# First layer's output product of four blocks as seven block products in phases of its own

## The chip, the cores and the metric

The kernel runs on one core of a Trainium2 chip. The metric is the device time of one execution in microseconds. Five engines of the core appear in the profile: TensorE (PE, with its weight loads as PEld), VectorE (DVE), ScalarE (ACT), GpSimd (POOL), SyncE (SP, which issues DMAs).

## The reference, cut to what matters

```python
def reference(**kw):
    attn = _attn_ref(q, k, v, mem_k, mem_v)              # batch 4, heads 8, sequence 768, head 64
    x = attn.transpose(0, 2, 1, 3).reshape(3072, 512)
    gate = 1.0 / (1.0 + np.exp(-(x @ w_gate)))            # first layer: 512 -> 1536 -> 512
    x = gate * (x @ w_val) @ w_out
    h = x @ w_in                                          # second layer: 512 -> 2048 -> 512
    P = a[0] + a[1] * h + a[2] * h**2 + a[3] * h**3
    Q = 1.0 + abs(b[0]) * abs(h) + abs(b[1]) * h**2
    return P / (Q + 1e-06) @ w_out2
```

The attention takes chunks of 32 queries with a context of 16 to the left and 8 to the right, and 8 memory keys in front. All is in fp32.

## The kernel before

An fp32 product is made of three matmuls in a shorter format: each operand is split into a high part (a ScalarE copy with rounding) and a low part (a VectorE subtraction), and TERMS multiplies high by high, high by low, low by high. A matmul takes 128x128 of weights and 512 columns of tokens. The 3072 tokens lie in six blocks of 512; the first layer's 1536 features in NF1 = 12 tiles of 128.

Every instruction goes through a `Recorder`, whose `emit` (line 485) is the line that all rows of the trace show; tiles tell them apart. `plan()` keeps TensorE's order as the code writes it, and sorts the instructions of ScalarE, VectorE and the DMA queues by costs and by due times counted back from the matmuls that need them. Each engine works its list in order.

Phase 1 does attention and the first layer of blocks 0 and 1 feature tile by feature tile: `gate_val`, then `out1(j, f)`, the output product ("visit") of one tile: 4 banks acc0 to acc3 x 3 terms = 12 matmuls, accumulating over the 12 tiles. Blocks (2, 3) and (4, 5) are then taken in pairs by `quads(ja, s0)`: for each of six feature pairs fp and for m = 0 (gate) and 1 (value), `quad` makes the 2 x 2 block product (two feature halves by two halves of tokens and of depth) with seven products for eight, by sums and differences of operands. A half is 7 products x 6 matmuls = 42. There are four PSUM banks for it (tiles p_fp_m_0 to 3); products 0 to 3 start a bank each, products 4, 5 and 6 add to banks 0, 2 and 3 after these have been read once. VectorE adds the banks up (u, v, c12, c21, c22); ScalarE takes the sigmoid; `done` multiplies by the gate: for block ja the result is split at once (`g_split`), for block jb it is kept unsplit (`g_held`) until later. Weights of the products are either plain ("a", from DRAM tensor wqa, split) or combined ("s", from wqs, where `w_comb_hi`, `w_comb_lo` and `w_comb_store` put them in split form, 512 KB each).

The visits of block ja stand between the halves (`visit(run)`, at all but the second half); those of block jb have a phase: for block 3 `outs(3, ...)`, mixed with attention of blocks 4 and 5; for block 5 the start of the second layer's task list: `visit1`, 10 of them pure (the last two of block 4 among them), and four inside the first three quads of the second layer, at the places LATE. A quad has two places for a visit, one ahead of its fifth product and one ahead of its last but one; filled are the first place of all three quads and the second of the third. The second layer takes three pairs of blocks, 8 quads each (tiles q_X, q_Y, q_Z).

## Time and profile before

| | us |
|---|---|
| Runs | 1134.87, 1133.35, 1133.77 (median 1133.77) |
| Span of the profiled execution | 1131.7 |
| Busy PE, DVE, ACT, POOL | 1120.1 (99%), 870.7 (77%), 746.8 (66%), 23.1 (2%) |
| DMA queue q1, share of 16 engines | 74.4% |
| Quads of blocks 2 and 3 | 254 to 402 |
| Output phase of block 3 | 402 to 453 |
| Quads of blocks 4 and 5 | 453 to 594 |
| Last visits of block 4, visits of block 5 | 594 to 624, the last four between 629 and 664 |
| Second layer | 624 to the end |

The runs are timed from outside the span, so they lie some 2 us above it. An engine's share is an average over stages; what an engine waits for in a stage is read from the timeline and the waits.

### The profile page before, as it was taken

To read this page: it belongs to the slowest core of one execution; us is meant where nothing else is said; L and a number is where in the kernel's file an instruction comes from. 1 tells how busy PE (TensorE), PEld (TensorE's weight loads), DVE (VectorE), ACT (ScalarE), POOL (GpSimd) and SP (SyncE) were. 2 spreads that over 40 slices of the span, in tenths; PEclk is the share of its full clock that TensorE was granted. 3 is DMA by queue.
4 is the path that set the end of the run, shared out by engine and by line. 5 is a ranking of instruction groups with operands and counts; after the bars stand their busy time and mean duration, and the time that the engine had idled before them with its cause. 6 is when DMAs were issued, how large, how long until landed. Compare 5 with 4: busy or idle time off the path is not lost.

```text
span 1131.7 us, 20049 instructions
## 1 busy us (share of the span) xinstructions
PE 1120.1 (99%) x7815; PEld 918.8 (81%) x7815; DVE 870.7 (77%) x1180; ACT 746.8 (66%) x1129; POOL 23.1 (2%) x39
## 2 busy tenths in 40 slices
PE   8999999999999999999999999999999999999998
PEld 4888888888888888888888788888888888888887
DVE  4788867764676767565667499999899999899982
ACT  5999565653355466343345599875799874898852
POOL 0000000000000000000000000000000000000000
PEclk8999999999999999999999999999999999999999
DMA  9899799997988899898967487679686689686682
GB/s 370 314 351 367 256 344 355 336 391 254 371 274 316 297 382 386 311 366 301 320 234 267 170 249 208 223 259 333 188 257 196 216 288 316 176 268 206 199 256 95
DMA packets 100319, 318.79 MB, mean 282 GB/s; under 512 B 10752, under 2 KB 11008, under 8 KB 100224
## 3 DMA queue, kind: packets, MB, share of 16 engines
q1 hardware_dynamic: 96192, 303.51, 74.4%
q0 software_dynamic: 3456, 12.58, 6.3%
q8 instruction: 62, 1.02, 0.4%
q10 hardware_dynamic: 576, 1.41, 0.3%
q14 instruction: 33, 0.27, 0.1%
HBM read 240.91 MB, written 63.96 MB: 269 GB/s over the span
## 4 chain that ended last, share of the span: by engine, by line
PE 95%; issue 2%; DMA 1%; ACT 1%; DVE 1%; POOL 0%; ACTq 0%; POOLq 0%; DVEq 0%
PE acc L485 40%; PE p L485 20%; PE h L485 12%; PE q_X L485 10%; PE q_Z L485 5%; PE q_Y L485 3%; PE xp L485 2%; PE sp L485 2%; PE tp L485 1%; DMA q<-u 1%; PE idle L485 1%; DMA k<-k_in 1%; ACT u L485 0%; DVE q L485 0%; DVE s L485 0%
## 5 line engine op out<-in xcount | busy, mean ns | idle before, releaser
L485 PE MATMUL acc<-w2o,G 128*128 128x512 f32 x1152 | 268.4, 389 | 0.0
L485 PEld LDWEIGHTS acc<-w2o,G 128*128 128x128 f32 x1152 | 216.3, 188 | 44.9
L485 PE MATMUL acc<-g,wp 128*128 128x512 f32 x720 | 177.2, 394 | 0.0
L485 PEld LDWEIGHTS acc<-g,wp 128*128 128x128 f32 x720 | 133.2, 188 | 28.7 <-issue 0.4
L485 PE MATMUL q_X<-x,wi 128*128 128x512 f32 x576 | 146.7, 390 | 2.2 <-ACT hb L485 2.0
L485 PE MATMUL p<-b,wpq_s 128*128 128x512 f32 x576 | 138.3, 389 | 0.0
L485 PE MATMUL h<-x,wp 128*128 128x512 f32 x576 | 137.5, 392 | 0.0
L485 PEld LDWEIGHTS q_X<-x,wi 128*128 128x128 f32 x576 | 107.8, 188 | 26.0 <-ACT hb L485 3.2
L485 PEld LDWEIGHTS p<-b,wpq_s 128*128 128x128 f32 x576 | 108.1, 188 | 22.5
L485 PEld LDWEIGHTS h<-x,wp 128*128 128x128 f32 x576 | 107.4, 188 | 22.4
L485 ACT ACTIVATE st<-st 128x512 f32<-128x512 f32 (+1 forms) x124 | 77.2, 673 | 0.0
L485 PE MATMUL p<-x,wpq_a 128*128 128x512 f32 x288 | 73.1, 389 | 0.0
L485 PE MATMUL q_Z<-x,wi 128*128 128x512 f32 x288 | 73.1, 389 | 0.0
L485 PEld LDWEIGHTS p<-x,wpq_a 128*128 128x128 f32 x288 | 54.1, 188 | 11.3
L485 PEld LDWEIGHTS q_Z<-x,wi 128*128 128x128 f32 x288 | 54.0, 188 | 11.3 <-DVE hb L485 0.2
L485 DVE SCALAR_TENSOR_TENSOR q<-q,u 128x1024 f32<-128x1024 f32 x48 | 58.4, 1219 | 3.9 <-ACT u L485 3.7
L485 DVE SCALAR_TENSOR_TENSOR t<-t,cf,u 128x1024 f32<-128x1024 f32 x48 | 61.4, 1279 | 0.1
L485 ACT ACTIVATE u<-q,qc 128x1024 f32<-128x1024 f32 x48 | 54.6, 1146 | 8.3 <-DMA q<-u 6.4
L485 ACT ACTIVATE G<-hb 128x512 fp32r<-128x512 f32 x48 | 29.9, 628 | 34.7 <-PE acc L485 29.4
L485 ACT ACTIVATE u<-u 128x1024 f32<-128x1024 f32 x48 | 50.3, 1055 | 0.4
L485 ACT ACTIVATE hb<-q_X 128x512 f32<-128x512 f32 x48 | 28.4, 592 | 32.0 <-PE q_X L485 32.0
L485 DVE TENSOR_TENSOR c<-u,p 128x512 f32<-128x512 f32 x39 | 26.8, 686 | 26.8 <-PE p L485 26.7
(290 smaller groups left out, 1703.4 us busy)
## 6 DMA issues: line engine op xcount, KB each, us to landing
w2o<-w2o SPq DMA_DIRECT2D x96, 512.0 KB, 4.6
wi<-wq SPq DMA_DIRECT2D x72, 512.0 KB, 4.8
st<-w_in SPq DMA_DIRECT2D x62, 512.0 KB, 6.8
wp<-wqa SPq DMA_DIRECT2D x55, 512.0 KB, 6.3
wpq_s<-wqs SPq DMA_DIRECT2D x48, 512.0 KB, 8.2
wpq_a<-wqa SPq DMA_DIRECT2D x36, 512.0 KB, 7.3
wqa<-wp SPq DMA_DIRECT2D x30, 512.0 KB, 6.8
v<-v_in SPq DMA_DIRECT2D x24, 512.0 KB, 6.3
```

Source lines behind the costliest of these rows:

```text
L485: getattr(getattr(self.nc, t.eng), op)(*[real(x) for x in args], **{n: real(x) for n, x in kw.items()})
```

## The change

The output product of blocks 2 to 5 is now taken per pair, as a 2 x 2 block product with seven products. The gated values of a pair are kept unsplit in four groups, "11", "12", "21", "22" (parity of the feature tile, block); `g_tile` gives them room. Each of the seven products (OUTS: the bank it goes to, the weights' slot, the operand) is taken in three steps k of four tiles, 12 matmuls each. A step is `o_weights` (one load of 512 KB), `o_split` (high part on ScalarE, low part on VectorE, 1024 columns each), for some `o_pre` (subtractions of 1024 columns that make the combined operands in place) and `o_mm`; `o_sum` copies or adds a bank when a product is done. X is the product that others continue in its banks.

Three steps (EARLY) run inside the quads, behind halves 5, 6 and 9. The other 18 (STEPS) come in an order of their own behind the quads: for blocks 2 and 3 with the attention of later blocks (`outs(2, O1, STEPS)`), for blocks 4 and 5 with 12 of them ahead of the second layer and six (LATE) at both places of its first three quads. Between the halves of the quads no visit is left, except the last one of block 1 and the three early steps.

The output weights are stored as eight slots per feature pair in a new tensor wqo; four of them are sums made in phase 1 (`o_whole`, `o_comb`, `o_store`). The combined gate and value weights go to wqs unsplit (256 KB); `w_comb_hi` and `w_comb_lo` are gone from phase 1, and each of the 48 loads in the quads is followed by its own high and low part. The steps of the attention for blocks 4 and 5 and of the second layer's weights have new places, and two tiles of x swap pools.

```diff
     def w_comb_store(i):
-        store_split(("s", i), wqs[i])
-        del wp["s", i]
+        nc.sync.dma_start(out=wqs[i], in_=sf[i])
...
-            src = wqa[2 * fp + w[1], w[2]] if w[0] == "a" else wqs[4 * fp + w[1]]
-            load_split(quad_key(ja, fp, w), src)
+            key = quad_key(ja, fp, w)
+            if w[0] == "a":
+                load_split(key, wqa[2 * fp + w[1], w[2]])
+                continue
+            t = split_tile(key)
+            hi, lo = t[:, 0], t[:, 1]
+            nc.sync.dma_start(out=lo.bitcast(F32), in_=wqs[4 * fp + w[1]])
+            nc.scalar.activation(out=hi, in_=lo.bitcast(F32), func=ACTF.Copy)
+            nc.vector.tensor_tensor(out=lo, in0=lo.bitcast(F32), in1=hi.bitcast(F32), op=ALU.subtract)
...
-            if j == jb:
-                nc.vector.tensor_tensor(out=g_held(j, f), in0=sg, in1=y, op=ALU.mult)
-                return
-            nc.vector.tensor_tensor(out=sg, in0=sg, in1=y, op=ALU.mult)
-            g_split((1, j, f), sg, 512)
+            o = f"{1 + f % 2}{1 + j - ja}"
+            nc.vector.tensor_tensor(out=g_held(ja, o, fp), in0=sg, in1=y, op=ALU.mult)
         tag = f"{ja}_{fp}_{m}"
         product(0)
...
         product(4)
         done(ja, f0, None)
         fill()
@@ -1023,18 +1035,25 @@
         add(c12, u, bank[2])
         done(jb, f0, c12)
         product(6)
-        c21 = t2(f"c21_{tag}")
-        add(c21, u, bank[3])
-        done(ja, f1, c21)
+        add(u, u, bank[3])
+        done(ja, f1, u)
...
+    def g_held(ja, o, fp):
+        return g_tile(ja, o, fp // 2)[:, fp % 2]
...
+    OUTS = (
+        ("X", 0, "11"),
+        ("Y", 2, "21"),
+        ("X", 4, "t2"),
+        ("Z", 5, "12"),
+        ("X", 7, "11"),
+        ("Z", 3, "21"),
+        ("X", 6, "22"),
+    )
+    ow, og, ob, osum = {}, {}, {}, {}
+    def flat(ap):
+        return ap.rearrange("p a n -> p (a n)")
+    def o_weights(ja, i, k):
+        t = ow[ja, i, k] = wpool.tile([P, 2, 512], F32R, tag="w", name=f"ow{ja}_{i}_{k}")
+        nc.sync.dma_start(out=t.bitcast(F32), in_=wqo[2 * k : 2 * k + 2, OUTS[i][1]].rearrange("f p n -> p f n"))
+    def o_sub(out, x0, x1):
+        nc.vector.tensor_tensor(out=flat(out), in0=flat(x0), in1=flat(x1), op=ALU.subtract)
+    def o_pre(ja, k, what):
+        for w in what:
+            if w == "1":
+                o_sub(g_tile(ja, "11", k), g_tile(ja, "12", k), g_tile(ja, "11", k))
+            elif w == "3":
+                o_sub(g_tile(ja, "12", k), g_tile(ja, "22", k), g_tile(ja, "12", k))
...
+    def o_split(ja, i, k):
...
+        hi, lo = (wpool.tile([P, 2, 512], F32R, tag="w", name=f"o{b}{ja}_{i}_{k}") for b in "hl")
+        nc.scalar.activation(out=flat(hi), in_=flat(src), func=ACTF.Copy)
+        nc.vector.tensor_tensor(out=flat(lo), in0=flat(src), in1=flat(hi).bitcast(F32), op=ALU.subtract)
+        og[ja, i, k] = hi, lo
+    def o_sum(ja, i, r):
+        tag = f"{ja}_{i}_{r}"
+        name, _, _ = OUTS[i]
+        bank = ob[ja, name, r]
+        def copy():
+            t = t2(f"os{tag}")
+            nc.scalar.activation(out=t, in_=bank, func=ACTF.Copy)
+            return t
+        def add(t):
+            nc.vector.tensor_tensor(out=t, in0=t, in1=bank, op=ALU.add)
+            return t
+        if i in (0, 2, 3):
+            osum[ja, i, r] = copy()
+        elif i == 1:
+            held.append((ja, r, add(osum.pop((ja, 0, r)))))
+        elif i == 4:
+            held.append((ja + 1, 2 + r, add(osum.pop((ja, 3, r)))))
+        elif i == 5:
+            held.append((ja, 2 + r, add(osum.pop((ja, 2, r)))))
+        else:
+            held.append((ja + 1, r, copy()))
+    def o_mm(ja, i, k):
+        name = OUTS[i][0]
+        w, x = ow.pop((ja, i, k)), og.pop((ja, i, k))
+        last = k == NF1 // 4 - 1
+        for r, f in ((r, f) for r in range(2) for f in range(2)):
...
+            for t, (a, b) in enumerate(TERMS):
+                c = 256 * a + P * r
+                nc.tensor.matmul(
+                    ob[ja, name, r],
+                    lhsT=w[:, f, c : c + P],
+                    rhs=x[b][:, f],
+                    start=(i in (0, 1, 3) and k == 0 and f == 0 and t == 0),
+                    stop=(last and f == 1 and t == 2),
+                    skip_group_check=True,
+                )
+            if last and f == 1:
+                o_sum(ja, i, r)
+    EARLY = [(0, 0), (1, 0), (0, 1)]
+    STEPS = [(0, 2), (1, 1), (1, 2)] + [(i, k) for i in range(2, len(OUTS)) for k in range(NF1 // 4)]
...
+    def o_whole(f):
+        t = so[f] = t2(f"so{f}")
+        hi, lo = (halves(wp[1, 1, f, 2], b).bitcast(F32) for b in range(2))
+        nc.vector.tensor_tensor(out=t.rearrange("p (m c) -> p m c", m=2), in0=hi, in1=lo, op=ALU.add)
+    def o_comb(fp):
+        t = [so.pop(2 * fp + i) for i in range(2)]
+        (a11, a21), (a12, a22) = ([x[:, 256 * m : 256 * m + 256] for m in range(2)] for x in t)
+        for out, x0, x1, op in (
+            (a22, a21, a22, ALU.add),
+            (a21, a11, a21, ALU.subtract),
+            (a11, a22, a11, ALU.subtract),
+            (a12, a12, a11, ALU.subtract),
+        ):
+            nc.vector.tensor_tensor(out=out, in0=x0, in1=x1, op=op)
+        for i in range(2):
+            split_out_hi(("so", fp, i), t[i])
+            split_out_lo(("so", fp, i), t[i])
+    def o_store(fp):
+        for i in range(2):
+            store_split(("so", fp, i), out_slots(fp, 4 + 2 * i))
+            del wp["so", fp, i]
...
+        EARLY_AT = dict(zip((5, 6, 9), EARLY))
+        def early(ja, i, k):
+            o_weights(ja, i, k)
+            o_split(ja, i, k)
+            o_pre(ja, k, "13" if i == 0 else "24x")
+            o_mm(ja, i, k)
         def quads(ja, s0):
             for i in range(NF1):
@@ -1474,35 +1621,41 @@
                 store1_end()
                 if m == 0 and fp < NF1 // 2 - 1:
                     quad_load(ja, fp + 1, 0, AHEAD)
-                if i:
-                    load_out(1 if fp < NF1 // 2 - 1 else 3)
                 run(*STORES)
                 run(*LOADS)
                 quad(ja, fp, m, lambda: run(attn_exp, conv2_hi, conv2_lo, conv2))
                 run(conv2_bits, comb2, pair_sum)
                 run(done2)
-                if i != 1:
-                    visit(run)
+                if (ja, i) == (2, 0):
+                    out1(*steps[-1])
+                if i in EARLY_AT:
+                    early(ja, *EARLY_AT[i])
+                run(pair_qk, pair_max)
                 run(pair_t)
-        def outs(j, s0, fn, n=NF1 + 1):
-            for i in range(n):
-                run = runner(s0 + i)
-                load_out(1)
+        def out_step(ja, i, k):
+            store1_end()
+            o_weights(ja, i, k)
+            if (i, k) == (2, 0):
+                o_pre(ja, k, "2")
+            o_split(ja, i, k)
+            if i < 2:
+                o_pre(ja, k, "13" if i == 0 else "24")
+            o_mm(ja, i, k)
+        def outs(ja, s0, steps):
+            for n, (i, k) in enumerate(steps):
+                run = runner(s0 + n)
                 run(quad_load)
                 run(*LOADS)
                 run(*STORES)
-                store1_end()
-                for nxt in visits[nv + 2 : nv + 3]:
-                    if nxt[0] == j:
-                        g_split((1, *nxt), g_held(*nxt), 512)
-                fn(i)
                 run(x_comb, attn_exp)
                 run(x_comb_hi, conv2_hi, conv2)
-                visit(run)
+                out_step(ja, i, k)
+                run(pair_out, pair_qk, pair_max)
                 run(pair_t)
                 run(x_comb_lo, conv2_lo, conv2_bits, comb2, pair_sum)
-                run(done2, conv2_keep)
+                run(done2)
...
-        outs(3, O1, lambda i: None)
+        outs(2, O1, STEPS)
         quads(4, Q2)
...
-        n5 = 10
-        for i, (j, f) in enumerate(todo1):
-            ready1(j, f)
-        for i, (j, f) in enumerate(todo1[:n5]):
-            visit1(j, f)
+        LATE = 6
+        for i, k in STEPS[: len(STEPS) - LATE]:
+            out_step(4, i, k)
         for i in range(4):
             load2i(0, 0, i)
-        late = list(todo1[n5:])
-        LATE = (4, 2, 0, 5, 3, 1)[: len(late)]
+        late = STEPS[len(STEPS) - LATE :]
...
-                    elif i in LATE:
-                        visit1(*late.pop(0))
+                    elif late:
+                        out_step(4, *late.pop(0))
+                        if not late:
+                            store1_end()
```

How the order moves shows at three places. The first is TensorE in the quads of blocks 4 and 5, at the seam between the two halves of the third feature pair (p_2_0 and p_2_1 are the banks, x and b the operands, wpq the weights). Before:

```order
L485 MATMUL p_2_0_2_5890<-b_5096,wpq_2_s_5809 128x512 x6
L485 MATMUL p_2_0_3_5907<-b_5279,wpq_2_a_1_5822 128x512 x6
L485 MATMUL acc_0_5740<-g_4_2_5836,wp_4_2_2_5473 128x512 x3
L485 MATMUL acc_1_5746<-g_4_2_5836,wp_4_2_2_5473 128x512 x3
L485 MATMUL acc_2_5753<-g_4_2_5836,wp_4_2_2_5473 128x512 x3
L485 MATMUL acc_3_5759<-g_4_2_5836,wp_4_2_2_5473 128x512 x3
L485 MATMUL p_2_1_0_5965<-x_0_4907,wpq_2_a_0_5712 128x512 x6
L485 MATMUL p_2_1_1_5976<-b_5121,wpq_2_s_5709 128x512 x6
```

and after:

```order
L485 MATMUL p_2_0_0_5868<-x_1_4869,wpq_2_a_1_5748 128x512 x6
L485 MATMUL p_2_0_2_5898<-b_5299,wpq_2_s_5745 128x512 x6
L485 MATMUL p_2_0_3_5912<-b_5407,wpq_2_a_1_5775 128x512 x6
L485 MATMUL p_2_1_0_5959<-x_0_4864,wpq_2_a_0_5697 128x512 x6
L485 MATMUL p_2_1_1_5972<-b_5199,wpq_2_s_5632 128x512 x6
L485 MATMUL p_2_1_2_5989<-b_5157,wpq_2_s_5628 128x512 x6
```

The visit of 12 matmuls (acc, with g and wp) is gone; the next half stands directly behind the one before.

The second is the end of the quads of blocks 4 and 5. On TensorE, before:

```order
L485 MATMUL p_5_1_0_6546<-x_1_4916,wpq_5_a_1_6350 128x512 x6
L485 MATMUL p_5_1_2_6577<-b_5096,wpq_5_s_6365 128x512 x6
L485 MATMUL p_5_1_3_6585<-b_5279,wpq_5_a_1_6389 128x512 x6
L485 MATMUL acc_0_5740<-g_4_9_6453,wp_4_9_2_6076 128x512 x3
L485 MATMUL acc_1_5746<-g_4_9_6453,wp_4_9_2_6076 128x512 x3
L485 MATMUL acc_2_5753<-g_4_9_6453,wp_4_9_2_6076 128x512 x3
L485 MATMUL acc_3_5759<-g_4_9_6453,wp_4_9_2_6076 128x512 x3
```

and after:

```order
L485 MATMUL p_5_1_0_6524<-x_1_4869,wpq_5_a_1_6349 128x512 x6
L485 MATMUL p_5_1_2_6550<-b_5299,wpq_5_s_6324 128x512 x6
L485 MATMUL p_5_1_3_6560<-b_5407,wpq_5_a_1_6374 128x512 x6
L485 MATMUL ob_X_6049<-oh_0_2_6600,ow_0_2_6463 128x512
L485 MATMUL ob_X_6049<-ol_0_2_6605,ow_0_2_6463 128x512
L485 MATMUL ob_X_6049<-oh_0_2_6600,ow_0_2_6463 128x512 x2
```

The visit of tile 9 stood behind the last half; now a step whose operand oh_0_2 and ol_0_2 come from the last half does.

On VectorE at the same place (v, c, u: sums of banks; gh: held gated values; g: those for a split), before:

```order
L485 TENSOR_TENSOR v_5_1_6592<-v_5_1_6592,p_5_1_3_6585 128x512
L485 TENSOR_TENSOR gh_2_6411<-c_4_5_0_6503,v_5_1_6592 128x512
L485 TENSOR_TENSOR c_4_5_0_6503<-c_4_5_0_6503,p_5_1_0_6546 128x512
L485 TENSOR_TENSOR c_4_5_1_6617<-p_4_5_1_6573,p_5_1_2_6577 128x512
L485 TENSOR_TENSOR g_4_10_6609<-c_4_5_0_6503,g_4_10_6609 128x512
L485 TENSOR_TENSOR gh_2_6411<-c_4_5_0_6520,c_4_5_1_6617 128x512
L485 TENSOR_TENSOR xf_0_1_0_6625<-p_4_5_1_6573,p_5_1_3_6585 128x512
L485 TENSOR_TENSOR c_4_5_0_6520<-c_4_5_0_6520,xf_0_1_0_6625 128x512
L485 TENSOR_TENSOR g_4_11_6641<-c_4_5_0_6520,g_4_11_6641 128x512
```

and after (ot, ol: combined operand and low part for the steps):

```order
L485 TENSOR_TENSOR v_5_1_6569<-c_4_5_0_6520,p_5_1_2_6550 128x512
L485 TENSOR_TENSOR ol_2_0_6571<-ot_0_6490,oh_2_0_6548 128x1024
L485 TENSOR_TENSOR v_5_1_6569<-v_5_1_6569,p_5_1_3_6560 128x512
L485 TENSOR_TENSOR ot_1_6580<-gh_22_0_5660,gh_11_0_5669 128x1024
L485 TENSOR_TENSOR gh_11_1_6418<-v_5_0_6498,p_5_1_0_6524 128x512
L485 TENSOR_TENSOR v_5_1_6569<-c_4_5_0_6520,p_5_1_2_6550 128x512
L485 TENSOR_TENSOR gh_22_1_6410<-v_5_0_6498,v_5_1_6569 128x512
L485 TENSOR_TENSOR gh_12_1_6435<-c_4_5_0_6520,v_5_1_6569 128x512
L485 TENSOR_TENSOR ol_0_2_6605<-gh_11_1_6418,oh_0_2_6600 128x1024
```

Operations of 1024 columns now stand between the sums, and the low part ol_0_2 behind the last products of the gate.

The third is TensorE in the second layer's second quad, before:

```order
L485 MATMUL q_1_Z<-x_0_3_6718,wi_1_1_6860 128x512 x6
L485 MATMUL q_1_X<-x_0_2_6735,wi_1_1_6860 128x512 x6
L485 MATMUL acc_5_0_6691<-G_5_9_6848,wv_9_6874 128x512 x3
L485 MATMUL acc_5_1_6699<-G_5_9_6848,wv_9_6874 128x512 x3
L485 MATMUL acc_5_2_6707<-G_5_9_6848,wv_9_6874 128x512 x3
L485 MATMUL acc_5_3_6713<-G_5_9_6848,wv_9_6874 128x512 x3
L485 MATMUL q_1_X<-x_0_1_6664,wi_1_2_6896 128x512 x6
L485 MATMUL q_1_X<-x_0_22_6743,wi_1_2_6896 128x512 x6
L485 MATMUL q_1_Z<-x_0_4_6749,wi_1_3_6918 128x512 x6
```

and after, from the second place on:

```order
L485 MATMUL q_1_X<-x_0_1_6753,wi_1_2_6945 128x512 x6
L485 MATMUL ob_X_6049<-oh_6_0_6909,ow_6_0_6950 128x512
L485 MATMUL ob_X_6049<-ol_6_0_6957,ow_6_0_6950 128x512
L485 MATMUL ob_X_6049<-oh_6_0_6909,ow_6_0_6950 128x512 x2
L485 MATMUL ob_X_6049<-ol_6_0_6957,ow_6_0_6950 128x512
L485 MATMUL ob_X_6049<-oh_6_0_6909,ow_6_0_6950 128x512
L485 MATMUL ob_X_6058<-oh_6_0_6909,ow_6_0_6950 128x512
L485 MATMUL ob_X_6058<-ol_6_0_6957,ow_6_0_6950 128x512
L485 MATMUL ob_X_6058<-oh_6_0_6909,ow_6_0_6950 128x512 x2
L485 MATMUL ob_X_6058<-ol_6_0_6957,ow_6_0_6950 128x512
L485 MATMUL ob_X_6058<-oh_6_0_6909,ow_6_0_6950 128x512
L485 MATMUL q_1_X<-x_0_22_6726,wi_1_2_6945 128x512 x6
```

Before, a visit stood at the first of the two places and none at the second, between q_1_X<-x_0_1 and q_1_X<-x_0_22; now a step stands at both.

## Rows read from the trace of the kernel before

**Rows 1.** The page: span, busy time of each engine, DMA in all.

```profile
span 1131.7 us, 20049 instructions
PE 1120.1 (99%) x7815; PEld 918.8 (81%) x7815; DVE 870.7 (77%) x1180; ACT 746.8 (66%) x1129; POOL 23.1 (2%) x39
...
DMA packets 100319, 318.79 MB, mean 282 GB/s; under 512 B 10752, under 2 KB 11008, under 8 KB 100224
```

**Rows 2.** The chain of waits, 263 to 297 us: start, length in us, what.

```profile
263.43 2.72 PE acc L485 x12
266.15 19.04 PE p L485 x84
285.19 2.72 PE acc L485 x12
287.91 9.52 PE p L485 x42
```

**Rows 3.** Stages: window, length, then busy us of PE, PEld, DVE, ACT, POOL, clock, DMA share, GB/s.

```profile
139.00:254.00 115.00, 115.00 (x1360) 95.28 (x1359) 82.00 (x128) 70.75 (x119) 0.34 (x2) 1.00 0.97 356
254.00:402.00 148.00, 148.00 (x1137) 122.07 (x1136) 97.41 (x145) 65.93 (x103) 0.49 (x3) 1.00 0.86 307
402.00:453.00 51.00, 51.00 (x714) 42.40 (x713) 35.08 (x57) 36.58 (x67) 0.00 (x0) 1.00 1.02 380
453.00:594.00 141.00, 141.00 (x624) 116.75 (x623) 82.83 (x138) 53.97 (x92) 0.00 (x0) 1.00 0.86 307
594.00:624.00 30.00, 30.00 (x134) 24.82 (x133) 22.88 (x37) 16.75 (x29) 0.00 (x0) 1.00 0.75 274
624.00:700.00 76.00, 73.96 (x324) 60.30 (x323) 60.29 (x62) 62.09 (x76) 3.62 (x4) 1.00 0.66 204
700.00:1100.00 400.00, 399.86 (x1765) 330.81 (x1764) 374.32 (x406) 316.63 (x399) 17.39 (x20) 1.00 0.75 241
```

**Rows 4.** TensorE's waits (total, times, longest), then its timeline at the second layer's start.

```profile
PE q_X L485 <- ACT hb L485: 2.0, 2, 1.4
...
634.37 1.65 PE L485 MATMUL q_X<-x,wi 128*128 128x512 f32 x6 [0.69 <-ACT hb L485]
...
648.26 1.67 PE L485 MATMUL q_X<-x,wi 128*128 128x512 f32 x6 [1.35 <-ACT hb L485]
```

**Rows 5.** Timeline of VectorE in the second layer: start, length in us, operation.

```profile
662.36 1.22 DVE L485 SCALAR_TENSOR_TENSOR q<-q,u 128x1024 f32<-128x1024 f32 x1
663.50 0.68 DVE L485 TENSOR_TENSOR hb<-hb,q_Z 128x512 f32<-128x512 f32 x1
664.10 1.28 DVE L485 SCALAR_TENSOR_TENSOR t<-t,cf,hb 128x1024 f32<-128x1024 f32 x1
```

**Rows 6.** Timeline of TensorE, the bare seam of blocks 2 and 3.

```profile
274.15 1.52 PE L485 MATMUL p<-b,wpq_a 128*128 128x512 f32 x6
275.51 1.52 PE L485 MATMUL p<-x,wpq_a 128*128 128x512 f32 x6
```

**Rows 7.** Timeline of all engines, at 404 and at 584 us.

```profile
404.53 1.03 PE L485 MATMUL tp<-ident,s 128*128 128x128 f32 x8
...
584.57 1.52 PE L485 MATMUL p<-x,wpq_a 128*128 128x512 f32 x6
...
586.12 0.60 ACT L485 ACTIVATE p<-p 128x512 f32<-128x512 f32 x1 [0.17 <-PE p L485]
```

**Rows 8.** Groups by shape: ScalarE's 1024-column pass (busy us, mean ns | idle before).

```profile
L485 ACT ACTIVATE u<-u 128x1024 f32<-128x1024 f32 x48 | 50.3, 1055 | 0.4
```

**Rows 9.** DMA issues: out<-in, count, KB each, median us to landing.

```profile
wi<-wq SPq DMA_DIRECT2D x72, 512.0 KB, 4.8
wi<-wq SPq DMA_DIRECT2D x24, 256.0 KB, 4.7
```

More of the change, by code (lines that the diff above doesn't have):

```diff
@@ L830, in split_lo, with halves, split_out_hi, split_out_lo @@
         nc.vector.tensor_tensor(out=t[:, 1], in0=src, in1=t[:, 0].bitcast(F32), op=ALU.subtract)
+    def halves(t, b):
+        return t.rearrange("p m (b c) -> p m b c", b=2)[:, :, b]
+    def split_out_hi(key, src):
+        t = split_tile(key)
+        nc.scalar.activation(out=halves(t, 0), in_=src.rearrange("p (m c) -> p m c", m=2), func=ACTF.Copy)
+    def split_out_lo(key, src):
+        hi, lo = (halves(wp[key], b) for b in range(2))
+        src = src.rearrange("p (m c) -> p m c", m=2)
+        nc.vector.tensor_tensor(out=lo, in0=src, in1=hi.bitcast(F32), op=ALU.subtract)
+    def out_slots(fp, i):
+        return wqo[fp, i : i + 2].rearrange("m p n -> p m n")
     def store_split(key, dst):
@@ L1134, in pv @@
         if n0 == 0 and (j < 2 or j % 2 == 0):
-            xt[j] = [x_tile(f"x{j}_{h}") for h in range(2)]
+            xt[j] = [
+                b_tile(f"x{j}_{h}", F32R, [P, 2, 2, 512]) if j >= 4 else x_tile(f"x{j}_{h}") for h in range(2)
+            ]
             if j >= 2:
@@ L1247, in fused_kernel @@
         at(s0, w_comb, i)
-        at(s0, w_comb_hi, i)
-        at(s0, w_comb_lo, i)
         at(s0 + 1, w_comb_store, i)
+    for f in range(NF1):
+        at(NF1 + f, o_whole, f)
+        if f % 2:
+            at(NF1 + f, o_comb, f // 2)
+            at(NF1 + f + 1, o_store, f // 2)
     for t in range(4, NPAIR, 2):
@@ L1452, in fused_kernel @@
             run(pair_sum)
-            run(w_comb_lo, x_comb_lo, conv2_lo, conv2_bits, comb2)
+            run(x_comb_lo, conv2_lo, conv2_bits, comb2)
             run(done2)
-        visits = [steps[-1]] + [(j, f) for j in range(PAIRS[0][0], NB1) for f in range(NF1)]
-        n_out, nv = 1, 0
-        def load_out(n):
-            nonlocal n_out
-            for v in visits[n_out : n_out + n]:
-                w1_load(*v, OUT)
-            n_out += n
-        def visit(run):
-            nonlocal nv
-            out1(*visits[nv], mid=lambda: run(pair_out, pair_qk, pair_max))
-            nv += 1
+        EARLY_AT = dict(zip((5, 6, 9), EARLY))
[4 more added lines that the diff above has]
+            o_mm(ja, i, k)
         def quads(ja, s0):
```

133 lines of the change are left out of this document (66 added, 67 removed).

## The prediction

> **What bounds the kernel now.** I read the page's busy table first: TensorE is busy 99% of the 1131.7 us span, VectorE 77%, ScalarE 66% [rows 1]. The chain of waits agrees; inside the quads it is nothing but TensorE work, 9.52 us for the 42 matmuls of a half and 2.72 us for the 12 of a visit, one straight behind the other [rows 2]. So a 512-column matmul costs 2.72 / 12 = 226.7 ns on the path that sets the end. The table by stage then tells what lies beside TensorE where the change works [rows 3]: in the quads of blocks 2 and 3 (254 to 402 us) VectorE is busy 97.4 of 148 us, in block 3's output phase (402 to 453) 35.1 of 51, in the quads of blocks 4 and 5 (453 to 594) 82.8 of 141, in block 5's visits (594 to 624) 22.9 of 30. TensorE is busy to the last hundredth in all four, at a granted clock of 1.00. The one place nearby where TensorE waits is the start of the second layer: 2.0 us in two waits for ScalarE [rows 4]. So a matmul taken away pays in full, as long as VectorE and the loads, which get more to do, keep up. Most of the working below is about that.
>
> **Removed: matmuls.** Of the 864 rows for the first layer's output product, 288 (blocks 0 and 1) stay. The four other blocks had 4 x 12 visits x 12 = 576; now two pairs have 7 products x 3 steps x 12 = 252 each, 504 in all. 72 matmuls fewer, 72 x 0.2267 = **-16.3 us** on the path. The gate and value matmuls (24 halves of 42) keep their number.
>
> **Added: VectorE's work.** Dense rows show that VectorE starts an operation of 1024 columns 1.14 us after the one before (662.36 to 663.50) though it lasts 1.22, and one of 512 columns 0.60 us after (663.50 to 664.10) though it lasts 0.68 [rows 5]. With these I count the operations of each stage from the order, wide and narrow ones, without the 128x1 ones:
> - Quads of blocks 2 and 3: 14 wide and 125 narrow before, 14 x 1.14 + 125 x 0.60 = 91 us (the trace has 97.4 busy with the overlap counted); after, 26 and 133, 109 us. TensorE has 148 us there now; eight visits go (three early steps come for eleven visits, and block 1's last visit stays), and the attention scores of a later stage come in, about 131 us. VectorE at 84%.
> - Output phase of blocks 2 and 3: 55 narrow, 33 us; after, 22 and 42, 50 us, beside 18 steps x 2.72 = 49 us of output products and some 15 us of attention. 78%.
> - Quads of blocks 4 and 5: 127 narrow, 76 us; after, 14 and 147, 104 us, beside 12 x 9.52 + 3 x 2.72 = 122.4 us. 85%; the tightest feature pair is the third, 22.0 us against 21.8.
> - From there to the first product of the second layer: 35 narrow, 21 us; after, 16 and 27, 34.4 us, beside 12 x 2.72 = 32.6 us.
> - Elsewhere small changes (the 12 output weights' sums and splits in the first phase, about 10 us, where VectorE has 82.0 of 115 [rows 3]).
>
> In all VectorE gets about 92 us more, some 960 of 1118. It is below TensorE in every stage but the fourth. I price this at nothing, except where the order makes TensorE wait. Cover if I am wrong there: none, every microsecond shows.
>
> **The seams between halves.** Before, a visit of 2.72 us lay between nearly all halves, and 2 seams were bare; after, 13 are, 5 in the first pair and 8 in the second. Both bare ones of before show no gap: the half that ends at 275.51 [rows 6], and the 84 matmuls in 19.04 us of the chain [rows 2]. What decides is when VectorE and ScalarE have read a bank that TensorE writes again. I walk through the tightest half (t = 0 at its first matmul, a product every 1.36 us) with VectorE's 0.60 and 1.14, and a reader that starts 0.17 us behind a product's end [rows 7]. Product 2 ends at 4.08 and could be read at 4.25; the operation ahead in VectorE's queue makes it 4.62, and the addition, lasting 0.68, ends at 5.30. Product 5 overwrites the bank from 6.80. Then comes a wide split (the change's new work), and the addition of product 3 starts at 4.62 + 0.60 + 1.14 = 6.36 and ends at 7.04; product 6 wants that bank at 8.16. The least margin is 1.1 us. Product 4's bank has from 6.80 to 9.52, the seam itself, to be read once by ScalarE. Bounds for the 13 seams: nothing (the two seams of before), or 13 x 0.69 = 9.0 to 13 x 1.35 = 17.6 us, by the two stalls at the second layer's start, where a visit between two products lacks too [rows 4]. I take **+2.0**: near the lower end, because the rows without a gap are the same kind of seam, and not at it, because VectorE is fuller than it was there.
>
> **Two handoffs at the phases' ends.** The first step after the last half needs a split of what that half has just made. At the end of blocks 4 and 5 (the order's second place): product 5 ends 1.36 us after product 4, VectorE reads it 0.17 later and then has three narrow operations ahead of the split's lower part, which lasts 1.22 [rows 5]: 1.36 + 0.17 + 3 x 0.60 + 1.22 = 4.55 us. TensorE wants it after products 5 and 6 and one matmul, at 2.72 + 0.23 = 2.95. **+1.6 us**, and about +0.3 at the step (1, 2) two steps later, whose split stands three wide operations behind. At the end of blocks 2 and 3 the same split ends at 5.09, but a transposition of 1.03 us [rows 7] stands between: **+1.1 us**. Below nothing these can't go; above, a 1.06 us pass of ScalarE [rows 8] could fall behind as well, +1 each. Before, the order put one whole visit (2.72 us) and the short split of 512 columns there, and no gap shows.
> After this VectorE works down its list to the last split for the second layer at 39.1 us, when TensorE wants it at 41.4: 2.3 us to spare.
>
> **Recovered.** The two waits at the second layer's start, 0.69 and 1.35 us [rows 4], stand inside a quad at its second place for a visit, where none is; the six late steps now lie at both places of the first three quads (the order's third place). **-2.0 us.**
>
> **Loads.** The combined weights come as 256 KB instead of 512, but the splitting pass follows, and a half-size load lands no sooner (4.7 against 4.8 us [rows 9]); they are asked for a feature pair ahead, so this is nothing. The queues carry less in the quads. In the output phase of blocks 2 and 3 some 20.4 MB must move in 65 us, 315 GB/s, and in block 5's old place some 12.5 MB in 35 us, 357 GB/s. Before, 380 GB/s at a DMA share of 1.02 went by without a TensorE gap (402 to 453) [rows 3]. Nothing; bounds 0 to +9 (below).
>
> **Sum.** 1131.7 - 16.3 - 2.0 + 1.6 + 0.3 + 1.1 + 2.0 = 1118.4 us of span. The median of the runs shown is 1133.77, 2.07 above the profiled span; so **1120.5 us**, 1.2% less.
>
> The saving itself has a second reading. The rows give 226.7 ns from matmul to matmul at 512 columns [rows 2]. The Trainium skill, "TensorE: Matmul & The Clock Gate", section "Wait — 56ns, not 53.3ns?", has 215.7 ns for back-to-back ones with a warm array; by that the removed matmuls would be worth 15.5 us and the time would be 1121.3. No row here is that fast, and the rows decide.
>
> **Rivals.**
> 1. *Bare seams cost what the second layer's did.* Each of the 13 stalls 0.69 us, 9.0 instead of 2.0: 1127.5 us. For it: those stalls are in the trace. Against it: there TensorE waits for ScalarE's copy in a longer chain, while the bare seam inside the quads shows none.
> 2. *VectorE in order holds the banks in every half; slower.* At 84 to 86% VectorE has little room for the order of its queue: one splitting pass put ahead of a bank's addition delays the bank. The gain is used up when each of the 24 halves loses (13.3 + 2.0) / 24 = 0.64 us, that is when VectorE is 1.1 + 0.64 = 1.74 us, three narrow operations, later than in my walk. At 0.69 each: 1120.5 - 2.0 + 16.6 = 1135.1 us. For it: the third feature pair, whose VectorE sum is above TensorE's. Against it: the list is made by due times, and elsewhere TensorE runs through 400 us with VectorE at 374 busy (700 to 1100 [rows 3]).
> 3. *VectorE's operations don't overlap.* Each costs its full 0.69 and 1.22 us, 0.08 more. In the stretch between the layers, 43 x 0.08 = 3.4 us, of which 2.3 are spare, and some 0.6 at each of the three handoffs: about +3, 1123.5 us. Against it, the dense starts of [rows 5]. The Trainium skill says the like in "VectorE: DVE Perf Modes", section "Terms": each operation is followed by a DRAIN, a flush, and the next can't issue until the pipe is empty. The starts 0.60 and 1.14 us apart, under operations recorded as longer, do not show it as an added time.
> 4. *The loads set the pace in the step phases.* If the transition's 12.5 MB go at the page's mean 282 GB/s [rows 1], they take 44 us and not 35: +9, 1129.5 us. Against it, 380 GB/s a stage before.
> 5. *The change doesn't shorten TensorE's path* (a step waits on an eviction each time its bank is used again): within 0.2% of before, 1133.
>
> **How the numbers follow.** Forecast 0.65; rival 1 0.13; rival 2 0.08; rival 3 0.06; rival 4 0.05; rival 5 0.03. What a measurement here can tell from no change is about 0.2%, 2.3 us: 1131.5 to 1136.0. Faster: the forecast, rivals 1, 3 and 4 but for a few hundredths, 0.87; the same: rival 5 and half of the nearer part of rival 2, 0.06; slower 0.07. The range: the seams at 0 and the handoffs at their least give 1120.5 - 2.0 - 3.0 = 1115.5; up to rivals 1 and 4, 1130. The forecast's own range is 1115.5 to 1124.
>
> **What would show it.** 7743 matmuls instead of 7815, and output products in steps of 12 matmuls and 2.72 us. In the waits of TensorE, a row on an output bank waiting for VectorE of 1 to 2 us, twice, and no more wait of q_X for hb in the first quads. VectorE's busy time up by some 90 us, the quads' windows with TensorE full. Wrong, if TensorE's waits show p for VectorE or ScalarE a dozen times or more (rivals 1 and 2), output products waiting for DMA (rival 4), or if the matmuls of the quads are spread without waits.

## The result, and the profile after

The changed kernel takes 1120.6 us (median of four runs, 1118.92 to 1120.86) against 1133.77: a ratio of 0.9878, 95% interval 0.9864 to 0.9892. Forecast was 1120.5. The profiled execution is the fastest of the four (1118.92 us, span 1117.1); the other three lie at 1120.5 to 1120.9. That matters below, where parts are added up to the profiled span.

The page, as in [rows 1]:

```profile
span 1117.1 us, 20117 instructions
PE 1104.8 (99%) x7743; PEld 905.7 (81%) x7743; DVE 954.3 (85%) x1284; ACT 777.7 (70%) x1159; POOL 23.1 (2%) x39
```

72 matmuls fewer, TensorE still at 99%, VectorE 83.6 us up. The stages, with the columns of [rows 3] (quads of blocks 2 and 3; their output steps; quads of blocks 4 and 5; the 12 steps ahead of the second layer):

```profile
254.09:385.60 131.51, 131.51 (x1063) 108.21 (x1063) 113.02 (x169) 75.74 (x118) 0.49 (x3) 1.00 0.82 290
385.60:449.01 63.41, 62.23 (x764) 51.78 (x763) 54.00 (x67) 42.96 (x67) 0.00 (x0) 1.00 0.76 263
449.01:571.50 122.49, 122.40 (x541) 101.04 (x539) 106.51 (x167) 68.01 (x115) 0.00 (x0) 1.00 0.86 302
571.50:606.18 34.68, 33.49 (x145) 27.22 (x146) 34.11 (x46) 23.58 (x34) 0.00 (x0) 1.00 0.78 255
```

VectorE has 113.0 of 131.5 us, 54.0 of 63.4, 106.5 of 122.5 and 34.1 of 34.7, and only in the second and fourth does TensorE miss anything. The chain of waits, as in [rows 2], shows the bare seams:

```profile
254.09 9.52 PE p L485 x42
263.61 2.72 PE acc L485 x12
266.33 28.56 PE p L485 x126
...
449.01 57.12 PE p L485 x252
506.13 2.72 PE ob_X L485 x12
...
521.09 28.56 PE p L485 x126
```

A seam between two halves is bare when neither output product nor attention stands in it. 126 matmuls, three halves, go by in 28.56 us and 252, six halves, in 57.12: 226.7 ns each, no gap at any seam. What TensorE still waits for in these stages and behind them is short (its waits: total, times, longest):

```profile
PE ob_X L485 <- DVE ol L485: 2.2, 2, 1.2
...
PE q_X L485 <- ACT hA L485: 0.7, 1, 0.7
...
PE ob_X L485 <- ACT oh L485: 0.3, 1, 0.3
```

Two waits for a low part ol and one for a high part oh are the handoffs, the places where a phase's first step needs what the phase before made last; the waits of q_X for hb in [rows 4] are gone. A wait of q_X for ScalarE's hA, at 941 us in the second layer, is new.

Stage by stage, with the borders put at the first and last matmul of the quads, the profiled execution goes from 148.05 to 132.00 us (first quads), 50.84 to 62.92 (output phase), 141.45 to 122.40 (second quads), 29.91 to 34.77 (up to the second layer), 507.70 to 511.08 (second layer; the six late steps instead of four visits are 5.4 of that), and +0.18 ahead of all: -14.6 us of span.

### The profile page after: what moved, and what is told of

Same layout as the page of the kernel before. It is cut to its first block, busy times and chain, and to the rows that moved or that the text cites. A ratio compares the mean times of both kernels' runs of the same rounds, so it can differ in the third digit from the quotient of the medians.

```text
span 1117.1 us, 20117 instructions
## 1 busy us (share of the span) xinstructions
PE 1104.8 (99%) x7743; PEld 905.7 (81%) x7743; DVE 954.3 (85%) x1284; ACT 777.7 (70%) x1159; POOL 23.1 (2%) x39
## 3 DMA queue, kind: packets, MB, share of 16 engines
q10 hardware_dynamic: 576, 1.41, 0.3%
## 4 chain that ended last, share of the span: by engine, by line
PE 84%; issue 12%; DVE 1%; DMA 1%; ACT 1%; POOL 0%; POOLq 0%; ACTq 0%
PE acc L485 22%; PE p L485 19%; PE h L485 12%; PE q_X L485 9%; PE ob_X L485 6%; PE q_Z L485 4%; PE ob_Z L485 3%; PE xp L485 2%; PE q_Y L485 2%; PE sp L485 2%; PE ob_Y L485 2%; PE tp L485 1%; DMA q<-u 1%; PE idle L485 1%; DMA k<-k_in 0%
## 5 line engine op out<-in xcount | busy, mean ns | idle before, releaser
L485 PEld LDWEIGHTS q_X<-x,wi 128*128 128x128 f32 x576 | 108.0, 188 | 23.7 <-ACT hA L485 1.1
L485 PE MATMUL acc<-g,wp 128*128 128x512 f32 x288 | 72.1, 394 | 0.0
L485 PEld LDWEIGHTS q_Z<-x,wi 128*128 128x128 f32 x288 | 54.1, 188 | 11.2
L485 PE MATMUL ob_X<-oh,ow 128*128 128x512 f32 x192 | 62.3, 392 | 0.3 <-ACT oh L485 0.3
L485 PEld LDWEIGHTS acc<-g,wp 128*128 128x128 f32 x288 | 53.1, 188 | 11.5
L485 ACT ACTIVATE u<-u 128x1024 f32<-128x1024 f32 (+1 forms) x57 | 55.9, 988 | 5.4 <-DVE u L485 4.9
```

The costliest lines, as they stand in the source:

```text
L485: getattr(getattr(self.nc, t.eng), op)(*[real(x) for x in args], **{n: real(x) for n, x in kw.items()})
```

## Experiments

**The changed kernel again.**

> The changed kernel once more, nothing altered, as the mark for the others of this round. Its four runs lay between 1118.92 and 1120.86 us, the profiled one lowest. All theories: 1120.6, within 1. TensorE's waits as before: ob_X for VectorE's ol twice, about 1.2 and 1.0 us, and 0.3 for ScalarE's oh.

1120.12 us (1119.41 to 1120.83), ratio 0.9875, 0.9861 to 0.9888. The profiled execution (span 1118.8) has the same three handoff waits to the hundredth, 1.18, 0.25 and 1.01, and 1.25 for hA instead of 0.72; its first quads take 132.60 instead of 132.00, most of it in 18 matmuls at 321 us that take 4.83 us instead of 4.26. So the handoffs belong to the kernel, and what sets one execution of it apart from another is elsewhere.

**The pure price of 72 matmuls.**

```diff
+                if j > 1 and i == 1 and (d == 0 or (d == 1 and f % 2)):
+                    continue
...
+                        if not second and t == 1 and (m == 0 or (m == 1 and k % 2)):
+                            continue
```

> The kernel before with 72 matmuls of the output product of blocks 2 to 5 left out (the second of the three terms, for one or two of the four banks of each visit), so that part of the product is missing; all else is as before. Theory: TensorE is the bound everywhere in these stages, so 72 x 0.2267 = 16.3 us go: 1117.5. That is the pure price of the removal, and the changed kernel then pays some 3 us for the rest. Rival: VectorE or the loads take part in the bound, so that fewer than 16.3 go: say 8 us, 1126.

One of the three terms is left out for one bank of each visit, and for a second bank in every other one. 1119.95 us (1118.72 to 1122.46), ratio 0.9876, 0.9863 to 0.9890: 14.2 us instead of 16.3. The stages tell why. From the second quads to the second layer 32 of the 72 go, 7.25 us by the row, and the stages shrink by 7.23 (141.45 + 29.91 to 138.06 + 26.07). In the first quads and their output phase 34 go, 7.7 us, and 6.7 are seen, beside a new wait of 0.94 us in the attention. The rest is lost in the second layer, in this profiled execution (the slowest of its runs) to a wait of 3.02 us at the same place where the changed kernel waits 0.72. Its row, with what stands before it (start, length, [idle before]):

```profile
929.53 0.87 POOL L485 DMA_DIRECT2D q<-u  x1 [24.19 <-PE acc L485]
...
940.61 1.15 ACT L485 ACTIVATE u<-q,qc 128x1024 f32<-128x1024 f32 x1 [6.41 <-DMA q<-u]
...
942.76 0.58 ACT L485 ACTIVATE hA<-q_X 128x512 f32<-128x512 f32 x1
943.39 1.08 PE L485 MATMUL q_X<-x,wi 128*128 128x512 f32 x3 [3.02 <-ACT hA L485]
```

GpSimd issues an accumulating DMA q<-u at 929.5; it lands 11.0 us later, and until then ScalarE stands in its queue at u, with the copy hA behind it that would free TensorE's bank. Behind this wait TensorE ran slower for a while too: the granted clock is 0.66 from 943 to 948 us, between its levels of 2.4 and 1.2 GHz, and nine matmuls there start up to 0.427 us apart instead of 0.227, which costs 1.6 us in all. So the matmuls pay in full in the second of these stages and nearly so in the first, and part of it is given back far away. The DMA is the sixteenth of 24 of its kind; it takes 10.0 and 10.1 us in the two profiles of the changed kernel, and 7.5 in the kernel before. Why it is longer is not shown.

**Handoffs: another step first.**

```diff
-    STEPS = [(0, 2), (1, 1), (1, 2)] + [(i, k) for i in range(2, len(OUTS)) for k in range(NF1 // 4)]
+    STEPS = [(1, 1), (0, 2), (1, 2)] + [(i, k) for i in range(2, len(OUTS)) for k in range(NF1 // 4)]
```

> The first two steps behind each pair's quads change places: first (1, 1), whose operand has long been there, then (0, 2), whose split comes from the last half. Theory: the handoff waits (1.18 + 1.01 + 0.25 us in the profile) come from a split that is 4.55 us behind product 4 while TensorE wants it at 2.95; with 2.72 us of other work ahead TensorE wants it at 5.67, and all three waits go: 2.4 us less, 1118.2. Rival: the waits are VectorE's lag as a whole, not of this one split; then the same time is lost a step later, and the run stays at 1120.6.

1119.67 us (1117.42 to 1124.61), ratio 0.9877, 0.9858 to 0.9897; against the 1120.12 of the run beside it that is no difference in so wide a spread. But the waits are clear. Both waits of ob_X are gone; in blocks 4 and 5 the step (1, 2), now third, waits in their place, for a low part and 0.3 us for a high part:

```profile
PE ob_Y L485 <- DVE ol L485: 1.3, 1, 1.3
```

Theory and rival each had half: in the first pair the wait was of that one split (its quads and steps take 194.2 us instead of 194.9), in the second VectorE is so far behind that the next split is late too (157.2 us to the second layer, as after).

**Late steps at the old places.**

```diff
-        LATE = 6
+        LATE = 4
...
-                    elif late:
+                    elif late and i in (0, 2, 4, 5):
```

> Only four late steps, at the places at which the kernel before had its four visits, so that the second place of the first two quads of the second layer is empty again; the other two steps go ahead of the second layer. Theory: TensorE waits there again for ScalarE's copy hb, 0.69 and 1.35 us: 2.0 us more, 1122.6, with two waits of q_X for hb. Rival: those waits came from work that blocks 4 and 5 no longer have, not from the empty places: 1120.6 and no such wait.

1122.73 us (1121.54 to 1123.76), ratio 0.9899, 0.9884 to 0.9914: 2.6 more than beside it. The waits are back, at the second place of the first two quads, 0.69 us each:

```profile
PE q_X L485 <- ACT hb L485: 1.4, 2, 0.7
```

**The weight part alone, on the kernel before.**

```diff
-        store_split(("s", i), wqs[i])
-        del wp["s", i]
+        nc.sync.dma_start(out=wqs[i], in_=sf[i])
...
-            src = wqa[2 * fp + w[1], w[2]] if w[0] == "a" else wqs[4 * fp + w[1]]
-            load_split(quad_key(ja, fp, w), src)
+            key = quad_key(ja, fp, w)
+            if w[0] == "a":
+                load_split(key, wqa[2 * fp + w[1], w[2]])
+                continue
+            t = split_tile(key)
+            hi, lo = t[:, 0], t[:, 1]
+            nc.sync.dma_start(out=lo.bitcast(F32), in_=wqs[4 * fp + w[1]])
+            nc.scalar.activation(out=hi, in_=lo.bitcast(F32), func=ACTF.Copy)
+            nc.vector.tensor_tensor(out=lo, in0=lo.bitcast(F32), in1=hi.bitcast(F32), op=ALU.subtract)
...
-        at(s0, w_comb_hi, i)
-        at(s0, w_comb_lo, i)
...
-            run(attn_qk, attn_max, conv2_hi, conv2, w_comb_hi, x_comb_hi)
+            run(attn_qk, attn_max, conv2_hi, conv2, x_comb_hi)
...
-            run(w_comb_lo, x_comb_lo, conv2_lo, conv2_bits, comb2)
+            run(x_comb_lo, conv2_lo, conv2_bits, comb2)
...
-            wqs = dp.tile([2 * NF1, P, 2, 512], F32, name="wqs")
+            wqs = dp.tile([2 * NF1, P, 512], F32, name="wqs")
```

> The kernel before with the weight part of the change alone: combined gate and value weights stored whole (256 KB) and split behind each load; the output product is as before. Theory: priced at nothing, since TensorE hides it: 1133.8 within 0.7, with 12 us or so more of VectorE and ScalarE each. Rival: the split behind the load makes the first combined weight of each feature pair late by its 1.2 us: 12 x 1.2 = 14 us more, 1148, with waits of p for VectorE's wpq.

1140.62 us (1139.91 to 1143.15), ratio 1.0062, 1.0047 to 1.0077: 6.6 us slower than the 1134.0 beside it, neither nothing nor 14. In its profile the first phase is 2.6 us longer, half of it before the first gate matmul, the output phase of block 3 1.05 (a wait of the attention), the second quads 1.7 and the second layer 1.0. Only the third comes near the expected kind, once, and its wait is for c and not for wpq:

```profile
495.81 0.68 DVE L485 TENSOR_TENSOR wpq_s<-wpq_s 128x512 fp32r<-128x512 f32 x1
...
497.93 0.69 DVE L485 TENSOR_TENSOR wpw<-c,wpw 128x512 fp32r<-128x512 f32 x1
...
498.71 0.69 DVE L485 TENSOR_TENSOR g<-c_s,g 128x512 fp32r<-128x512 f32 x1
499.32 1.28 DVE L485 TENSOR_TENSOR c<-u,p 128x512 f32<-128x512 f32 x2
500.05 1.19 PE L485 MATMUL p<-b,wpq_a 128*128 128x512 f32 x4 [1.41 <-DVE c L485]
```

A low part of a loaded weight (wpq_s), two low parts for stores and operands (wpw, g) stand ahead of the sum c in VectorE's queue, and the matmul that overwrites c's bank waits 1.41 us. The changed kernel has none of these waits; its tables of steps differ from the old ones too. What makes the first phase longer here stays open, and so does how much of the 6.6 us comes from the split and how much from the new order.

**VectorE's margin.** The margin of a half is the time between the end of the addition that reads a bank and the product that overwrites it. One, two and three more operations are put into each half, between the additions of bank 2 and bank 3 (one is shown). `plan()` lays VectorE's list anew for each of these kernels, so that they differ from the changed kernel in more than the added operations:

```diff
+        for _ in range(1):
+            nc.vector.tensor_tensor(out=v, in0=v, in1=v, op=ALU.max)
```

> The changed kernel with one more operation of 512 columns on VectorE in each of the 24 halves, in the chain between the additions of bank 2 and bank 3 (it changes no value). Theory: the least margin in the walk is 1.1 us and the operation takes 0.60; VectorE gets 7.2 us more beside 122.5 us of TensorE in blocks 4 and 5, where it has 106.5: at most 1 us more, 1120.6 to 1121.6. Rival (VectorE holds the banks already): 24 x 0.60 = 14.4 us more, 1135.

1122.27 us (1118.56 to 1122.96), ratio 0.9898, 0.9882 to 0.9915: 2 us more than the changed kernel's by the medians, while the profiled execution, the fastest, is no slower than that one's (1118.56 and 1118.92). Two halves of 24 wait for v, and one a little for c:

```profile
PE p L485 <- DVE v L485: 1.0, 2, 0.8
```

These are not the halves that had least to spare. In one of them two wide operations now stand beside the added one (v<-v) ahead of bank 3's addition (v<-v,p), where the changed kernel has one narrow operation:

```profile
544.63 1.22 DVE L485 TENSOR_TENSOR gh<-gh,gh 128x1024 f32<-128x1024 f32 x1
545.77 0.68 DVE L485 TENSOR_TENSOR v<-v 128x512 f32<-128x512 f32 x1
546.37 1.22 DVE L485 TENSOR_TENSOR gh<-gh,gh 128x1024 f32<-128x1024 f32 x1
547.51 0.68 DVE L485 TENSOR_TENSOR v<-v,p 128x512 f32<-128x512 f32 x1
```

> Two more operations of 512 columns between the additions of bank 2 and bank 3 in each half. One cost 1.7 us in all, three cost 58. If the margin of a half decides: 1.2 us more against 1.1 of room, so a few tenths in a half at most, with one or two tighter ones: 4 to 10 us more, 1124 to 1130. If the sum on VectorE decides (106.5 + 14.4 = 121 beside 122.5 in blocks 4 and 5, 127 beside 131.5 in blocks 2 and 3): nothing beyond the run with one, 1122.

1136.47 us (1133.93 to 1138.62), ratio 1.0023, 1.0014 to 1.0033: 16 us more, and slower than the kernel before. The quads take some 9 us longer in each pair than after; in 16 of the 24 halves TensorE waits ahead of the last product, the one that overwrites bank 3. Two of the rows:

```profile
PE p L485 <- DVE v L485: 7.3, 8, 1.9
PE p L485 <- DVE u L485: 3.2, 5, 1.0
```

> The same with three such operations in each half. Theory: bank 3 is read 1.8 us later, 0.7 past the margin of 1.1, and VectorE's sum goes to 128 us against 122.5 and to 135 against 131.5: it becomes the bound, 9 to 17 us more, 1129 to 1137, with waits of p for VectorE. Rival (the queue has much more room than the walk says): 1120.6.

1178.37 us (1176.14 to 1180.85), ratio 1.0391, 1.0375 to 1.0407: 58 us more, far past the 9 to 17. The two stretches of the quads:

```profile
254.00:412.00 158.00, 140.63 (x1071) 111.51 (x1070) 138.41 (x210) 79.07 (x122) 0.49 (x3) 0.97 0.74 249
474.00:627.00 153.00, 132.19 (x539) 104.79 (x538) 131.03 (x210) 69.00 (x116) 0.00 (x0) 0.95 0.74 247
```

and the largest of the four rows of TensorE's waits for it:

```profile
PE p L485 <- DVE v L485: 27.2, 15, 3.5
```

The quads are 25 and 32 us longer than after; 38 us of that are such waits, in 22 of the 24 halves, up to 3.5 us each. VectorE isn't full (138.4 of 158): it waits for TensorE's products in its turn. And TensorE is slower in between: a granted clock of 0.97 and 0.95 in these stretches. Its busy time is 19 us more than in the same quads after. Some 11 of these are 53 matmuls that start 0.427 us apart instead of 0.227, the level of 1.2 GHz instead of 2.4. They stand in eight places, each right behind a wait of 2.0 to 3.5 us; one such place:

```profile
528.25 2.26 PE L485 MATMUL p<-b,wpq_a 128*128 128x512 f32 x6 [2.16 <-DVE v L485]
530.31 2.55 PE L485 MATMUL p<-x,wpq_a 128*128 128x512 f32 x6
```

Behind the other 14 waits, of 0.2 to 2.0 us, there are none, and none in the run with two operations, whose longest wait is 1.9 us.

The same three operations behind the last sum of a half, where no bank waits for them:

```diff
+        for _ in range(3):
+            nc.vector.tensor_tensor(out=u, in0=u, in1=u, op=ALU.max)
```

> The same three operations of 512 columns in each half as in the run with three, but behind its last sum, where no bank and no result waits for them. If their place in the chain between two banks made the 58 us: VectorE's sum alone counts, 128 us beside 122.5 and 135 beside 131.5, about 9 us more, 1130, or up to 15 with the phases behind. If VectorE's sum made them: again 1178.

1134.73 us (1129.49 to 1137.82), ratio 1.0000, 0.9985 to 1.0014: 14 us more, a quarter of 58 for the same work, though in a list that was laid anew as well. The stretches (quads, steps, quads, steps) of the profiled execution, one of the slowest of ten:

```profile
254.09:391.48 137.39, 134.21 (x1065) 109.82 (x1064) 127.27 (x195) 76.48 (x118) 0.49 (x3) 0.99 0.81 275
391.48:458.28 66.80, 64.27 (x761) 52.44 (x760) 59.77 (x78) 42.62 (x67) 0.00 (x0) 0.97 0.76 258
458.28:582.28 124.00, 122.97 (x542) 101.20 (x540) 119.65 (x188) 64.57 (x109) 0.00 (x0) 1.00 0.86 294
582.28:618.19 35.91, 33.54 (x145) 26.80 (x144) 35.91 (x54) 23.77 (x34) 0.00 (x0) 1.00 0.77 244
```

The second quads run with VectorE busy 119.7 of 124.0 us and cost 1.6 us more than after. The first cost 5.4 more, 2.8 of it in one wait of an early step for its split; the first steps cost 3.9 and the second layer 6.6. So the backlog comes out where a step needs a split, and in the second layer, at a clock of 0.97 in the first step phase and 0.72 from 624 to 630 us:

```profile
PE ob_X L485 <- DVE ol L485: 3.4, 4, 1.4
PE ob_Y L485 <- DVE ol L485: 3.1, 2, 2.8
```

**No early steps.**

```diff
-    EARLY = [(0, 0), (1, 0), (0, 1)]
-    STEPS = [(0, 2), (1, 1), (1, 2)] + [(i, k) for i in range(2, len(OUTS)) for k in range(NF1 // 4)]
+    EARLY = []
+    STEPS = [(0, 0), (1, 0), (0, 1), (0, 2), (1, 1), (1, 2)] + [(i, k) for i in range(2, len(OUTS)) for k in range(NF1 // 4)]
...
-                o_pre(ja, k, "13" if i == 0 else "24")
+                o_pre(ja, k, "13" if i == 0 else "24x" if k == 0 else "24")
```

> The changed kernel without the three early steps inside each pair's quads: all 21 steps come behind the quads, so that every seam of the second pair is bare and VectorE has 105 us beside 114 of TensorE there (92%). Theory: a bare seam costs nothing and VectorE still has its margin: 1120.6 within 1. Rival: at 92% the order makes the banks late, a few tenths in most halves: 1124 to 1128, with waits of p for VectorE.

1115.70 us (1114.85 to 1119.27), ratio 0.9844, 0.9828 to 0.9860: faster than the changed kernel by 4 to 5 us, which was not expected. All 21 steps of a pair now stand behind its quads. The chain shows why it isn't slower:

```profile
447.82 114.24 PE p L485 x504
562.06 2.72 PE ob_X L485 x12
564.78 2.72 PE ob_Y L485 x12
567.50 5.44 PE ob_X L485 x24
```

504 matmuls in 114.24 us: all twelve halves of the second pair stand bare, VectorE at 89% (101.8 us busy), without a gap. Then the first step is (0, 0), whose operand was made in the first halves, and its matmuls follow straight on. No handoff wait is left. Once more:

> The kernel without early steps once more, to fix its time. The stage lengths of its first profile say that both handoffs are gone, 194.9 to 193.6 us up to the second pair and 157.2 to 155.0 from there to the second layer, 3.5 us together; so 1116.5 to 1117 if that is all. Rival: the whole difference of the first medians, 4.7 us, 1115.7.

1115.68 us (1115.16 to 1118.35), ratio 0.9842, 0.9827 to 0.9856. This kernel beats both. Its stages account for 1.6 us (first quads with their phase, 194.92 to 193.35) and 2.1 (second quads to the second layer, 157.17 to 155.04), 3.7 in all, about what the handoffs had cost, 3.3 and a slower first matmul behind each wait; the last microsecond of the medians is not settled.

## Why the forecast came out

The time is within 0.1 us of the forecast, and that is in part luck: two terms were off and cancelled against things that the sum didn't have.

**Removed, -16.3: right.** The matmuls are gone at 226.7 ns each. The run with the matmuls alone left out shows 7.23 of 7.25 us in two of the stages. The quads keep this pace in the changed kernel too: 57.12 / 252 is 226.7 again. The Trainium skill's 215.7 ns ("TensorE: Matmul & The Clock Gate", section "Wait — 56ns, not 53.3ns?") is not reached by these products. The forecast's words that no row is that fast hold for the rows it shows, not for the whole trace: bf16 matmuls of 512 columns that the kernel issues at its start (tile idle, 9.9 to 12.1 us after) follow each other at 215.8 ns.

**VectorE, nothing outside the handoffs: right, with the count a tenth too high.** It got 83.6 us more, not 92 (15.6, 18.9, 23.7 and 11.2 in the four stages against 18, 17, 28 and 13); the terms that the count lists add up to 87. The margin of 1.1 us in the walk is nearly what the changed kernel's trace has. In its 24 halves the addition of bank 3 ends 0.95 to 1.83 us ahead of product 6, and the least is in the third feature pair, as forecast, behind a wide split:

```profile
492.33 1.22 DVE L485 TENSOR_TENSOR ol<-gh,oh 128x1024 fp32r<-128x1024 f32 x1
493.46 0.68 DVE L485 TENSOR_TENSOR v<-v,p 128x512 f32<-128x512 f32 x1
495.09 1.52 PE L485 MATMUL p<-b,wpq_a 128*128 128x512 f32 x6
```

By these margins alone one operation of 0.60 us would make no half wait, and two (1.2) three halves, by some 0.3 us at most. The runs show two or three halves and 16: the rest comes from the new order of the list or from delays that carry on from one half to the next, and no run here tells these apart.

**Seams, +2.0: mis-sized, they cost 0.** Rival 1 falls: 6 halves in a row, and 12 without early steps, go through at the matmuls' own pace. The price was taken from the second layer's start, where another chain decides (q_X needs a copy from ScalarE).

**Handoffs, 1.6 + 0.3 + 1.1: right in place and nearly in size.** In the timeline at the end of the second quads (after), product 5 begins at 568.53, when product 4 ends:

```profile
568.53 1.52 PE L485 MATMUL p<-b,wpq_s 128*128 128x512 f32 x6
569.89 1.52 PE L485 MATMUL p<-b,wpq_a 128*128 128x512 f32 x6
570.09 0.69 DVE L485 TENSOR_TENSOR v<-c,p 128x512 f32<-128x512 f32 x1
570.70 0.69 DVE L485 TENSOR_TENSOR gh<-v,v 128x512 f32<-128x512 f32 x1
571.30 0.69 DVE L485 TENSOR_TENSOR gh<-c,v 128x512 f32<-128x512 f32 x1
571.67 0.49 PE L485 MATMUL ob_X<-oh,ow 128*128 128x512 f32 x1 [0.25 <-ACT oh L485]
571.90 1.22 DVE L485 TENSOR_TENSOR ol<-gh,oh 128x1024 fp32r<-128x1024 f32 x1
...
573.17 0.50 PE L485 MATMUL ob_X<-ol,ow 128*128 128x512 f32 x1 [1.01 <-DVE ol L485]
```

VectorE reads bank 2 at 570.09, 1.56 behind (walked: 1.53); the operations follow 0.61 and 0.60 apart, the low part starts at 571.90, and TensorE goes on at 573.17, 4.64 behind product 4 (walked: 4.55). TensorE would have wanted it at 571.25 + 0.23 = 571.48, so 1.69 us are lost (1.6), of which the profile names 0.25 and 1.01. At the first pair it goes on at 388.38 instead of 386.95: 1.4 (1.1). Of the +0.3 at the step (1, 2) 0.17 is there, too short for a row of its own: its first matmul with a low part starts at 578.91, 0.40 behind the one before instead of 0.23. It came up as 1.3 where TensorE hadn't waited ahead of it (the order with (1, 1) first). Rival 3 falls with the starts 0.60 apart under operations of 0.69: the Trainium skill's line in "VectorE: DVE Perf Modes", section "Terms", that the next operation can't issue until the pipe is empty, doesn't show here as added time.

**Recovered, -2.0: right.** Put back, the empty places cost 2.6 us of the time, 1.4 of it in two waits of q_X for hb; the rest was not traced.

**Loads, nothing: right for the changed kernel** (second step phase at a DMA share of 0.78, 255 GB/s, no wait for DMA), so rival 4 falls. Its estimate of the bytes was too high, though: 255 GB/s over 34.68 us are 8.8 MB and not 12.5. And the weight part alone costs 6.6 us on the old order, so the price of nothing holds for the change as a whole, whose order was made anew; which part of the new order does it was not tested.

**Rival 2 was the one to fear.** Its mechanism is real and near: three operations later was the turning point that it named, and two are enough to make the kernel slower than before (1136.5). How it goes on was underestimated: with three, waits of 38 us came and some 11 us of lower clock on top. That a late bank delays VectorE's next input, and so adds to itself, would fit, but is not shown apart from the new order. Rival 5, no gain, falls with the time itself.

**What the sum lacked:** q_X's wait for hA in the second layer, 0.7 to 1.2 us in the profiles of the changed kernel, 0.1 in the one before. With it, handoffs of 3.3 and seams of 0, the sum is 1131.7 - 16.3 - 2.0 + 3.3 + 0.7 = 1117.4 us, beside the profiled span of 1117.1. The median lies 1.7 above the profiled execution, and that made up for the 2.0 of the seams.

## What to carry to other kernels

Where TensorE is full, price a removed matmul at the spacing in its own stage, and look for the loss not at seams whose reader has time but where a phase's first operand is made by the last phase's last product: start with a step whose operand is old. For an engine that works its list in order, the busy share says little; what counts is by how much each result comes ahead of the instruction that overwrites its source. Read that margin from the trace, and test it by putting operations into the chain: here 89% busy was free, while two operations of 0.60 us more in each half cost more than the change had won. Where a planner orders the queue, look at the order as well, since an added operation moves others.
